# Global scores moved behind the local scores, on eight 64x32 parts, in the steady part of an attention and feed-forward kernel

## The chip, the cores and the metric

The kernel runs on one core of one Trainium2 chip (trn2). The metric is the device time of one execution in microseconds, lower is better. A core has TensorE (PE) for matmuls, with the loading of weights shown as an engine of its own (PEld), VectorE (DVE), ScalarE (ACT), GpSimd (POOL), and SyncE (SP), which issues the transfers.

## The reference

Attention over 8 batches and 8 heads with head size 64: 512 local tokens, which see the local keys within a window of 32 on either side and the 32 global keys, and 32 global tokens, which see all 544 keys. Its output is the input of a feed-forward stage with token shift (an RWKV channel mix), in float32.

```python
k_all = np.concatenate([k_g, k_l], axis=2)
v_all = np.concatenate([v_g, v_l], axis=2)
s_g = scale * np.matmul(q_g, k_all.transpose(0, 1, 3, 2))
out_g = np.matmul(sm(s_g), v_all)
...
s_l = np.concatenate([s_lg, s_ll], axis=-1)      # s_ll masked to the window
out_l = np.matmul(sm(s_l), np.concatenate([v_g, v_l], axis=2))
...
xk = mu_k * x + (1.0 - mu_k) * x_prev
xr = mu_r * x + (1.0 - mu_r) * x_prev
k = np.maximum(xk @ w_k, 0.0)
v = k * k @ w_v
r = 1.0 / (1.0 + np.exp(-(xr @ w_r)))
return r * v
```

## The kernel before

A unit is a batch and two neighbouring heads on 128 partitions (64 per head); two units make a pair, and a batch of eight heads is two pairs. The keys stand in 22 blocks of 32 (`ORDER`): after every three local blocks comes a copy of the global keys, so that a window of 128 columns holds three local blocks and the global one. The feed-forward stage multiplies float32 operands as two parts, high and low, in three products (`products`, L615). A feed-forward step is 24 matmuls of 256 columns into one PSUM bank (2 halves, 4 blocks, 3 products), or as many with the values' weights.

PSUM has eight banks. In the middle of the kernel (`MIDDLE_USE`, L132) three are used in turn under the name "m", four under "s" and one under "t". The feed-forward stage uses "m"; the local scores, weighted sums and part of the transposes use "s"; transposes and the smaller part of the global scores use "t".

The opening (`FIRST`, L66) is a list of steps by hand for batches 0 and 1 and the softmax of the first pair of batch 2; the pairs in it are called a to e. From batch 1 on `in_turn` (L970) takes turns, by a string of letters (`BATCH`, L1365), between attention steps ("A", for the pairs of the next batch) and feed-forward steps ("F"). The order of TensorE's instructions is that of the program (`in_line`), and so are those of VectorE, ScalarE and GpSimd (`manual_schedule`, L1209). Waits for tiles and banks are put in by the framework.

The attention steps of a pair are in `attention` (L925): transposes of the local probabilities of this pair, transposes of its global probabilities in two groups (`transposes_global`, L530), and behind the second group, in the same step, the local scores of the next pair (`scores`, L434, per unit: `make` L383 with 64 matmuls in all per pair on parts of 64 rows and 32 columns, then `read` L404 on VectorE). One or more feed-forward steps follow. The next attention step begins with the next pair's global scores (`Global.make`, L479): queries of both heads in a block-diagonal 128x64 operand, one matmul of 480 columns and one of 64 per unit, so that the two units stand on partitions 0 to 63 and 64 to 127. `Global.read` (L495) has VectorE take the smallest of the negated scores per row and copy. Behind that stand the weighted sums of this pair (`weighted`, L549; 56 matmuls of two passes). `exps`, `norm` and `soften` (L965) spread the exponentials and normalizations of the softmax over the feed-forward steps that follow.

A matmul of float32 operands appears in the trace as two instructions; the feed-forward parts are of type fp32r, and appear as one.

## Time and profile before

| | before |
|---|---|
| median of 3 runs | 630.09 us (629.71 to 630.24) |
| profiled execution, first to last instruction | 628.5 us |
| busy: TensorE | 620.1 us (99%) |
| busy: VectorE | 440.0 us (70%) |
| busy: ScalarE | 379.7 us (60%) |
| busy: GpSimd | 340.1 us (54%) |

The profiled execution is known by its span; what the runs' times hold beyond it (1.6 us of the median) lies before the first and behind the last instruction. Names in the rows are those of the program: `ps_s`, `ps_t` and `ps_m` are the banks, `raw_qk` holds a unit's queries and keys, `Pt` and `Pg` the local and global probabilities, `PT` their transposes, and `raw_v` the values. A matmul's line is that of a helper (L160 for matmuls, L163 for transposes), so blocks are told apart by tiles and shapes: 64*32 is a matmul on 64 rows and 32 columns of the array, and 128x480 moves 480 columns.

### The profile page before, as it was taken

The numbers are of one execution on the slowest core, as the hardware profiler recorded it, in microseconds if no ns is written. First come the engines' busy times: TensorE is split into PE (matmuls) and PEld (weight loads), VectorE is DVE, ScalarE is ACT, GpSimd is POOL, SyncE is SP. The second block draws the span as 40 slices with busy tenths as digits, with TensorE's granted clock in tenths as the row PEclk, the third lists the DMA queues.
The fourth block names the chain that finished last, engine by engine and source line by source line (L and its number), as shares of the span: only waits on it lengthen the run. The fifth ranks groups of instructions, "written<-read, shape, count | busy, mean of one in ns | idle before, by whom it ended". The sixth has DMA issues, their size and how long they took to land.

```text
span 628.5 us, 20469 instructions
## 1 busy us (share of the span) xinstructions
PE 620.1 (99%) x8356; PEld 590.7 (94%) x8356; DVE 440.0 (70%) x1227; ACT 379.7 (60%) x1147; POOL 340.1 (54%) x310
## 2 busy tenths in 40 slices
PE   8999999999999999999999999999999999999997
PEld 4689999999999999999999999999999999999997
DVE  7999983758888487676695677676696657345960
ACT  6899967164383768565857657665847744433531
POOL 8786455536846245846276535846275534543660
PEclk9999999999999999999999999999999999999999
DMA  8955562457383546276463928276463834377684
GB/s 337 408 197 217 193 224 82 169 183 273 118 305 131 201 139 236 60 269 235 158 248 108 378 75 335 88 267 228 162 243 104 299 117 137 105 222 246 200 261 142
DMA packets 43278, 127.29 MB, mean 203 GB/s; under 512 B 3760, under 2 KB 20656, under 8 KB 43184
## 3 DMA queue, kind: packets, MB, share of 16 engines
q1 hardware_dynamic: 43184, 125.98, 56.1%
q8 instruction: 66, 1.08, 0.7%
q14 instruction: 28, 0.23, 0.1%
HBM read 108.66 MB, written 17.30 MB: 200 GB/s over the span
## 4 chain that ended last, share of the span: by engine, by line
PE 85%; DVE 5%; DMA 3%; POOL 3%; ACT 2%; issue 1%; DVEq 0%; POOLq 0%; ACTq 0%
PE ps_m L160 65%; PE ps_s L160 13%; PE ps_t L163 4%; PE ps_t L160 2%; DMA w<-w_v 2%; ACT Pt L417 1%; PE ps_s L163 1%; DMA raw_qk<-qk 1%; POOL wv_l L271 1%; DVE a L299 1%; DVE diff L664 1%; POOL w L252 1%; POOL Pt L428 0%; DVE diff L659 0%; DVE xfull L664 0%
## 5 line engine op out<-in xcount | busy, mean ns | idle before, releaser
L160 PE MATMUL ps_m<-xkh,wk_h 128*128 128x256 f32 x544 | 154.1, 283 | 0.0
L160 PE MATMUL ps_m<-xkl,wk_h 128*128 128x256 f32 x544 | 150.5, 277 | 0.0
L160 PE MATMUL ps_m<-xkh,wk_l 128*128 128x256 f32 x544 | 150.5, 277 | 0.0
L160 PE MATMUL ps_m<-bh,a 128*128 128x256 f32 x736 | 131.7, 278 | 0.0
L428 POOL TENSOR_TENSOR Pt<-Pt,ssum 128x512 f32<-128x512 f32 x64 | 69.4, 1088 | 81.0 <-ACT Pt L417 38.9
L160 PEld LDWEIGHTS ps_m<-bh,a 128*128 128x128 f32 x736 | 113.1, 188 | 0.0
L417 ACT ACTIVATE Pt<-Pt,m 128x128 f32<-128x128 f32 x256 | 99.5, 395 | 14.4 <-DVE m L410 14.4
L160 PEld LDWEIGHTS ps_m<-xkh,wk_h 128*128 128x128 f32 x544 | 102.2, 188 | 3.7 <-issue 1.2
L160 PEld LDWEIGHTS ps_m<-xkh,wk_l 128*128 128x128 f32 x544 | 102.3, 188 | 0.0
L160 PEld LDWEIGHTS ps_m<-xkl,wk_h 128*128 128x128 f32 x544 | 102.2, 188 | 0.0
L160 PE MATMUL ps_m<-bl,a 128*128 128x256 f32 x368 | 101.7, 276 | 0.0
L160 PE MATMUL ps_m<-xrh,wr_h 128*128 128x256 f32 x272 | 76.7, 282 | 0.0
L702 ACT ACTIVATE relu<-ps_m 128x512 f32<-128x512 f32 x52 | 30.9, 595 | 74.3 <-PE ps_m L160 69.0
L669 POOL TENSOR_TENSOR xkl<-xfull,xkh 128x512 fp32r<-128x512 f32 x30 | 40.2, 1339 | 65.8 <-DVE ssum L361 33.6
L160 PE MATMUL ps_m<-xrl,wr_h 128*128 128x256 f32 x272 | 75.2, 277 | 0.0
L160 PE MATMUL ps_m<-xrh,wr_l 128*128 128x256 f32 x272 | 75.2, 276 | 0.0
L410 DVE CUSTOM_DVE_ANT_0 Pt<-ps_s,masks 128x128 f32<-128x128 f32 x256 | 55.9, 285 | 24.2 <-PE ps_s L160 24.2
L160 PEld LDWEIGHTS ps_m<-bl,a 128*128 128x128 f32 x368 | 69.2, 188 | 0.0
L669 POOL TENSOR_TENSOR xrl<-diff,xrh 128x512 fp32r<-128x512 f32 x30 | 41.5, 1383 | 41.8 <-DVE xrh L668 26.7
L788 DVE TENSOR_TENSOR bl<-B,bh 128x512 fp32r<-128x512 f32 x41 | 40.1, 992 | 27.6 <-ACT bh L787 27.4
L788 POOL TENSOR_TENSOR bl<-B,bh 128x512 fp32r<-128x512 f32 x35 | 47.8, 1387 | 19.1 <-ACT bh L787 11.4
L664 DVE SCALAR_TENSOR_TENSOR diff<-diff,mu_r_sb,xT 128x256 f32<-128x256 f32 x56 | 57.2, 1061 | 0.0
(154 smaller groups left out, 1477.3 us busy)
## 6 DMA issues: line engine op xcount, KB each, us to landing
a<-scratch SPq DMA_DIRECT2D x92, 512.0 KB, 4.8
raw_v<-v SPq DMA_DIRECT2D x32, 896.0 KB, 8.6
raw_qk<-qk SPq DMA_DIRECT2D x32, 628.0 KB, 5.0
out_l<-gate SPq DMA_DIRECT2D x32, 256.0 KB, 2.2
w<-w_k SPq DMA_DIRECT2D x8, 512.0 KB, 12.9
w<-w_v SPq DMA_DIRECT2D x8, 512.0 KB, 4.0
w<-w_r SPq DMA_DIRECT2D x4, 512.0 KB, 3.6
scratch<-wv_h SPq DMA_DIRECT2D x8, 256.0 KB, 2.7
```

What stands on the lines that cost most here:

```text
L160: return in_line(nc.tensor.matmul(*a, **kw))
L163: return in_line(nc.tensor.transpose(*a, **kw))
L252: nc.gpsimd.tensor_scalar(word(n, F32, 1), word(n, F32, 1), REBIAS, 1.0, op0=ALU.mult, op1=ALU.mult)
L271: nc.gpsimd.tensor_sub(part_of_weights(n, "l"), word(n, F32, 0), part_of_weights(n, "h").bitcast(F32))
L299: nc.vector.tensor_sub(s.bitcast(F32R), s, hs.bitcast(F32))
L410: nc.vector.tensor_tensor_reduce(out=self.Pt[:, i], in0=self.place(t, n, h), in1=masks[:, 2 * self.slots[t][1] + n], op0=ALU.add, op1=ALU. ...
L417: nc.scalar.activation(self.Pt[:, i], self.Pt[:, i], AF.Exp, bias=self.low_x[:, i:i + 1], scale=-1.0, accum_out=self.ssum[:, i:i + 1],)
L428: nc.gpsimd.tensor_mul(self.Pt[:, some], self.Pt[:, some], inv.unsqueeze(2).to_broadcast([P, 4, W]))
L664: nc.vector.scalar_tensor_tensor(self.shape(xf[:, j]), self.shape(d[:, j]), mu[:, c0 + j:c0 + j + 1], self.prev(c0 + j), op0=ALU.mult, op1 ...
L669: nc.gpsimd.tensor_sub(lo[:, both], xf, hi[:, both].bitcast(F32))
L702: nc.scalar.activation(rk, kp, AF.Relu)
L788: (by or (nc.vector if b[0] == "B" else nc.gpsimd)).tensor_sub(l, val, h.bitcast(F32))
```

## The change

From the second pair of batch 2 on (eleven pairs), the global scores are made by a new class, `GlobalByHalves`, directly behind the local scores of both units, in the same attention step; the feed-forward steps that stood between them now stand between the scores and the weighted sums alone. The keys are taken in two halves, and heads apart: a matmul has the 64 rows of one head, the 32 queries of one unit, and first 192, then 128 columns of keys, so eight matmuls of a round stand on eight different parts. The rows of a head's bank are then half, unit and query; the heads are in two banks, one under "t" and one under "m". The 128-column round overlaps between the halves and is masked with a constant (`twice`). Since a row's keys are in two partitions' rows, `both` combines the smallest values and the sums of the halves. The exponentials, normalizations and copies of the transposes are done per head; the transposes of the second group go to an "m" bank. VectorE's reads stand in the order: first unit's first bank, its second bank, the global scores, the second unit's two banks. The first pair keeps the old code. A few tiles get padding: `Pg` by 512 bytes, `twice` 1024 bytes, `other` 128 bytes in each of four buffers.

```diff
--- before.py
+++ after.py
@@ -52,6 +52,7 @@
 )
 QG = 2 * SG
+GK = 2 * (W - CK) + W
 K0 = QG + SL
 NV = 2 * NW * D
 TOK = 256
@@ -197,6 +198,7 @@
     nothing = const.tile([P, SL - CK], BF16, name="nothing")
     nc.gpsimd.memset(nothing, 0.0)
+    twice = const.tile([P, 512], BF16, name="twice")[:, :GK]
     PT = const.tile([P, 2, 2, PART], F32, name="PT")
@@ -493,9 +495,9 @@
                 matmul(out[j * QG:(j + 1) * QG], s.qk[:, 0:QG], keys, start=True, stop=True)
         def read(self):
-            self.Pg = att2.tile([P, NGK], F32, tag="Pg", name="Pg")
+            self.Pg = att2.tile([P, NGK + P], F32, tag="Pg", name="Pg")[:, :NGK]
             self.m = small.tile([P, 2], F32, tag="mg", name="mg")
-            self.ssum = small.tile([P, 1], F32, tag="ssumg", name="ssumg")
+            self.ssum = small.tile([P, 2], F32, tag="ssumg", name="ssumg")[:, 0:1]
             nc.vector.tensor_tensor_reduce(
                 out=self.Pg[:, FIRST_K:], in0=self.sp[1], in1=nothing[:, :NGK - FIRST_K], op0=ALU.add, op1=ALU.min,
                 scale=-scale, scalar=HUGE, accum_out=self.m[:, 0:1],
@@ -517,6 +519,87 @@
         def norm(self):
             self.inverse()
             self.normalize()
+    class GlobalByHalves:
+        def __init__(self, units):
+            self.units = units
+        def make(self):
+            self.sp = [psum("t"), psum("m")]
+            for at, n in ((0, 2), (2 * (W - CK), 1)):
+                for u, s in enumerate(self.units):
+                    for half in range(2):
+                        first = s.k[:, 2 * W * half:2 * W * half + W - CK] if n == 2 else (
+                            s.k[:, SK - W:] if half == 0 else s.k[:, SK - CK - W:SK - CK]
+                        )
+                        out = slice((2 * half + u) * SG, (2 * half + u + 1) * SG)
+                        for h in range(2):
+                            rows = slice(h * D, (h + 1) * D)
+                            keys, to = first[rows], self.sp[h][out, at:at + n * first.shape[1]]
+                            if n == 2:
+                                keys = bass.AP(keys.tensor, keys.offset, (keys.ap[0], (W, 2), (1, W - CK)))
+                                to = to.rearrange("p (t n) -> p t n", t=2)
+                            matmul(to, s.qk[rows, h * SG:(h + 1) * SG], keys, start=True, stop=True)
+        def both(self, x, op, tiny):
+            other = small.tile([P, 32], F32, tag="other", name="other")[:, :2]
+            for half in range(2):
+                there = x[(1 - half) * D:(2 - half) * D]
+                nc.vector.tensor_tensor(other[half * D:(half + 1) * D], there, there, op=ALU.max)
+            if tiny is None:
+                nc.vector.tensor_tensor(x, x, other, op=op)
+            else:
+                nc.vector.scalar_tensor_tensor(x, x, tiny, other, op0=ALU.add, op1=op)
+        def read(self):
+            self.Pg = att2.tile([P, NGK + P], F32, tag="Pg", name="Pg")[:, :2 * GK].rearrange("p (h n) -> p h n", h=2)
+            self.m = small.tile([P, 2], F32, tag="mg", name="mg")
+            self.ssum = small.tile([P, 2], F32, tag="ssumg", name="ssumg")
+            for h in range(2):
+                nc.vector.tensor_tensor_reduce(
+                    out=self.Pg[:, h], in0=self.sp[h][:, :GK], in1=twice, op0=ALU.add, op1=ALU.min,
+                    scale=-scale, scalar=HUGE, accum_out=self.m[:, h:h + 1],
+                )
+            self.both(self.m, ALU.min, None)
+        def exps(self):
+            for h in range(2):
+                nc.scalar.activation(
+                    self.Pg[:, h], self.Pg[:, h], AF.Exp, bias=self.m[:, h:h + 1], scale=-1.0,
+                    accum_out=self.ssum[:, h:h + 1],
+                )
+        def norm(self):
+            self.both(self.ssum, ALU.add, 1e-9)
+            nc.vector.reciprocal(self.ssum, self.ssum)
+            for h in range(2):
+                nc.gpsimd.tensor_scalar(
+                    self.Pg[:, h], self.Pg[:, h], self.ssum[:, h:h + 1], 1.0, op0=ALU.mult, op1=ALU.mult
+                )
+    def transposes_by_halves(Pg, h):
+        tp = psum("tm"[h])[:, :3 * P].rearrange("p (t n) -> p t n", n=P)
+        for n, at in enumerate((0, W - CK, 2 * (W - CK))):
+            size = W if n == 2 else W - CK
+            transpose(tp[:size, n], Pg[:, h, at:at + size], ident)
+        def place(rows, at, step, n):
+            first = PT[rows, 0, h, at:at + CK]
+            return bass.AP(first.tensor, first.offset, (first.ap[0], (step, n), (2 * PART, 2), (1, CK)))
+        for rows, half, ns, at, step in (
+            (slice(0, W - CK), 0, slice(0, 2), TAIL[0], TAIL[1] - TAIL[0]),
+            (slice(0, W - CK), 1, slice(0, 3), TAIL[2], CK),
+            (slice(D, P), 0, slice(2, 3), TAIL[5], CK),
+        ):
+            n = ns.stop - ns.start
+            nc.scalar.copy(
+                place(rows, at, step, n),
+                tp[rows, ns, half * D:(half + 1) * D].rearrange("p t (u q) -> p t u q", u=2),
+            )
     def cells(x, at, step, n, size=CK):
@@ -935,25 +1018,34 @@
                     for copy in done:
                         copy()
                     yield
-            transposes_global(Pg, 0)()
-            yield
-            transposes_global(Pg, 1)()
+            for part in range(2):
+                if pair is pairs[0]:
+                    transposes_global(Pg, part)()
+                else:
+                    transposes_by_halves(Pg, part)
+                if part == 0:
+                    yield
             if nxt:
-                R = [scores(whole(s)) for s in nxt]
+                R = [Scores(whole(s)) for s in nxt]
+                G = GlobalByHalves(nxt)
+                R[0].make()
+                R[0].read(0)
+                R[1].make()
+                G.make()
+                R[0].read(1)
+                G.read()
+                R[1].read(0)
+                R[1].read(1)
                 halves = list(product(R, range(2)))
                 halves[0][0].exps(0)
                 for (r, h), (r_next, h_next) in zip(halves, halves[1:]):
                     softmaxes.append((lambda r=r, h=h: r.norm(h), lambda r=r_next, h=h_next: r.exps(h)))
             yield
-            if nxt:
-                G = Global(nxt)
-                G.make("s", "t")
-                G.read()
-                Pg = G.Pg
             weighted(pair, True)()
             if nxt:
                 softmaxes.append((lambda: R[1].norm(1), G.exps))
                 softmaxes.append((G.norm,))
+                Pg = G.Pg
             for s in nxt or ():
                 load_v(s)
             yield pair[1].c + 1 == NC
@@ -1220,6 +1312,9 @@
         for s in pair_of["e"]:
             if not hasattr(s, "v"):
                 load_v(s)
+    nc.gpsimd.memset(twice, 0.0)
+    nc.gpsimd.memset(twice[:D, GK - W:GK - D], NEG)
+    nc.gpsimd.memset(twice[D:, GK - CK:], NEG)
     heads = attention(later_pairs, [group["e0"], group["e1"]], group_g["e"].Pg)
     leftp = sump = gate3 = None
     SUMS_AT = range(4, 20)
```

## Rows read from the trace of the kernel before

**Rows 1.** The page: span; TensorE busy time, share, instructions.
```profile
span 628.5 us, 20469 instructions
...
PE 620.1 (99%) x8356; PEld 590.7 (94%) x8356; DVE 440.0 (70%) x1227; ACT 379.7 (60%) x1147; POOL 340.1 (54%) x310
```

**Rows 2.** TensorE's waits, 126 to 500 us: total, times, longest.
```profile
PE ps_s L160 <- DVE m L410: 0.3, 1, 0.3
```

**Rows 3.** TensorE timeline, 474.7 to 478: start, length, line, operation, instructions.
```profile
475.42 2.06 PE L160 MATMUL ps_s<-raw_qk 64*32 64x128 f32 x128
477.40 0.38 PE L160 MATMUL ps_m<-xkh,wk_h 128*128 128x256 f32 x1
```

**Rows 4.** The same view, 482.6 to 488 us.
```profile
482.86 0.28 PE L160 MATMUL ps_m<-xkh,wk_l 128*128 128x256 f32 x1
483.06 0.34 PE L160 MATMUL ps_t<-raw_qk 128*64 128x64 f32 x4
483.23 0.98 PE L160 MATMUL ps_s<-raw_qk 128*64 128x480 f32 x4
484.03 3.63 PE L160 MATMUL ps_s<-PT,raw_v 128*64 128x96 f32 x112
487.59 0.39 PE L160 MATMUL ps_m<-xrh,wr_h 128*128 128x256 f32 x1
```

**Rows 5.** The same view, 516.9 to 521.5 us, the last pair.
```profile
517.28 0.28 PE L160 MATMUL ps_m<-xkh,wk_l 128*128 128x256 f32 x1
517.48 3.68 PE L160 MATMUL ps_s<-PT,raw_v 128*64 128x96 f32 x112
521.09 0.39 PE L160 MATMUL ps_m<-xrh,wr_h 128*128 128x256 f32 x1
```

**Rows 6.** Groups by form, 126 to 500: count, busy us, mean ns, idle.
```profile
L160 PE MATMUL ps_s<-raw_qk 128*64 128x480 f32 x44 | 10.8, 569 | 0.3 <-DVE m L410 0.3
```

**Rows 7.** TensorE timeline, 170.4 to 176.2 us, one pair.
```profile
171.00 0.34 PE L160 MATMUL ps_t<-raw_qk 128*64 128x64 f32 x4
171.60 1.03 PE L160 MATMUL ps_s<-raw_qk 128*64 128x480 f32 x4 [0.26 <-DVE m L410]
172.43 3.75 PE L160 MATMUL ps_s<-PT,raw_v 128*64 128x96 f32 x112
176.10 0.39 PE L160 MATMUL ps_m<-xkh,wk_h 128*128 128x256 f32 x1
```

**Rows 8.** Groups by form, 126 to 500 us, VectorE.
```profile
L410 DVE CUSTOM_DVE_ANT_0 Pt<-ps_s,masks 128x128 f32<-128x128 f32 x176 | 38.0, 285 | 21.9 <-PE ps_s L160 21.9
...
L503 DVE CUSTOM_DVE_ANT_0 Pg<-ps_s,nothing,mg 128x480 f32<-128x480 f32 x11 | 7.9, 718 | 2.7 <-PE ps_s L160 1.7
...
L361 DVE TENSOR_SCALAR ssum<-ssum 128x4 f32<-128x4 f32 x44 | 7.6, 173 | 3.4 <-ACT Pt L417 3.3
```

**Rows 9.** Groups by form, 126 to 500 us, ScalarE.
```profile
L509 ACT ACTIVATE Pg<-Pg,mg 128x544 f32<-128x544 f32 x11 | 8.1, 736 | 0.0
...
L540 ACT COPY PT<-ps_t 96x384 f32<-96x384 f32 x11 | 5.1, 465 | 0.0
```

**Rows 10.** Timeline of all engines, 294.5 to 304.5 us, VectorE and ScalarE.
```profile
294.60 0.69 DVE L888 TENSOR_TENSOR sum<-ps_m,sum 128x512 f32<-128x512 f32 x1 [0.83 <-PE ps_m L160]
...
297.66 0.60 ACT L702 ACTIVATE relu<-ps_m 128x512 f32<-128x512 f32 x1 [2.10 <-PE ps_m L160]
...
299.34 0.47 ACT L540 COPY PT<-ps_t 96x384 f32<-96x384 f32 x1
...
300.68 0.28 DVE L410 CUSTOM_DVE_ANT_0 Pt<-ps_s,masks 128x128 f32<-128x128 f32 x1
...
304.19 0.69 DVE L780 TENSOR_TENSOR B<-B,B 128x512 f32<-128x512 f32 x1
```

**Rows 11.** Engines by stretch: busy us (instructions) per engine, clock, DMA.
```profile
110.51:113.43 2.92, 2.92 (x28) 2.92 (x27) 2.88 (x7) 0.59 (x1) 0.00 (x0) 1.00 0.34 102
113.78:116.61 2.83, 2.83 (x28) 2.83 (x27) 2.73 (x5) 0.59 (x1) 1.23 (x1) 1.00 0.95 368
```

## The prediction

> **What bounds the kernel now.** I read the page first. Its first lines say that TensorE is busy for 620.1 of the 628.5 us of the span [rows 1]: this kernel ends when TensorE has got through its list, and the other engines count only where TensorE waits for them. So I looked at TensorE's waits next. In the stretch from 126 to 500 us, which holds all scores that the change touches, no wait on its list is longer than 0.3 us, and that one is for VectorE's reads of local scores [rows 2]. What is left to win is TensorE's own time. I therefore read its timeline block by block, always from the first start of one block to the first start of the next, because the modelled ends overlap.
>
> In a pair of units the local scores are 128 instructions (64 matmuls of two passes each) on eight 64x32 parts of the array, from 475.42 to 477.40 us [rows 3]. Two feed-forward steps later the global scores follow: 8 instructions on two 128x64 parts, from 483.06 to 484.03, and straight behind them the weighted sums, to 487.59 [rows 4]. The last pair has no global scores ahead of its weighted sums, so it shows what a feed-forward step followed directly by weighted sums costs: from 517.48 to 521.09 [rows 5]. The group of 480-column matmuls has 44 instructions in the stretch, four per block, so there are 11 such blocks [rows 6]. That is the number of pairs which the change touches; the earlier three pairs with this shape are in the hand-written opening and keep the old code.
>
> **Part by part: TensorE.** Removed, per pair: the block of global scores, 484.03 - 483.06 = 0.97 us [rows 4]. The 0.20 us between the last feed-forward matmul (482.86) and the block's first stays, for the weighted sums need the same change of parts: in the last pair it is 517.48 - 517.28 = 0.20 as well [rows 5]. What comes back is that the first weights of the sums are no longer loaded beside global scores: 3.61 us with no global block ahead [rows 5] against 3.56 with one [rows 4], so 0.05.
>
> Added, per pair: 16 matmuls of two passes, so 32 instructions, half of them on 192 columns and half on 128, behind the local scores and on the same eight parts. I take their pace from the local scores. Those take 1.98 us [rows 3], of which about 0.20 is the change back to the full array (as large as the 0.20 of [rows 4]), so 1.78 for 128 instructions: 13.9 ns for 128 columns on one of eight parts, or 0.87 ns for a column on one part (13.9 x 8 / 128). The old global block bears out that this is a rate of columns: two parts, each with 2 passes of 64 and 480 columns, 1088 columns in 0.97 us, or 0.89 ns each [rows 4]. The new block gives each part 2 x (192 + 128) = 640 columns: 640 x 0.88 = 0.56 us. Bounds: if the 13.9 ns were a rate of instructions, 32 x 13.9 = 0.45; if small matmuls cost what those of the weighted sums do, 3.36 us (3.56 less the change of parts) / 112 = 30 ns [rows 4], 32 x 30 = 0.96. I take 0.56, because these are the same kind of instruction on the same parts as in [rows 3], plus 0.02 once a pair, since the new code visits the four column parts in the order 0, 2, 1, 3 and the local scores in the order 0, 1, 2, 3. The change back to the full array is paid once, as now.
>
> The Trainium skill, page "TensorE: Matmul & The Clock Gate", section "Wait — 56ns, not 53.3ns?", has a rule against this change: start to start of matmuls is said never to fall under about 25 ns, however few columns they have. By it the new block would cost an estimated 32 x 25 = 0.8 us, and the gain would shrink to 0.12 us a pair, some 628.5 us in all. The trace does not agree for matmuls on separate parts: those of [rows 3] follow each other at 13.9 ns.
>
> The transposes of the global probabilities stay six per pair, with the same column sizes (two of 96 and one of 128 per group where they were 96, 96, 128 and 96, 96, 96); I cost this at nothing on TensorE.
>
> Net per pair: 0.97 - 0.05 - 0.56 - 0.02 = 0.34 us; for 11 pairs 3.7 us.
>
> **One pair is different.** At 171.00 the old global block takes 1.43 us (to 172.43) and its weighted sums 3.67 (to 176.10), because it needs a score bank that VectorE has not read yet: 0.46 and 0.11 us more than in a usual pair [rows 7]. VectorE reaches those reads late there, whatever TensorE does. In the new order no global matmul stands there, and the weighted sums come 0.6 us later to the same banks. They use three of the four banks of the local scores, in the order in which VectorE reads them; the third is read behind the new global reads (about 1.5 us, below), and may bring back up to 0.4 us. Of the 0.57 I count 0.3.
>
> **The other engines.** VectorE reads two banks of 320 columns instead of 64 and 480, and has three small operations more in the read and two more in the normalization. From 285 ns for 128 columns and 718 for 480 [rows 8], 320 columns take about 520 ns, some 0.45 from start to start; a small operation like the sum's takes 0.17 to 0.2. The new read is 2 x 0.45 + 3 x 0.2 = 1.5 us where the old was about 0.8, and with two more small operations VectorE gets about 1.1 us a pair. ScalarE gets six copies for three and two exponentials for one: with 465 ns for a copy of 384 columns and 736 for the exponential of 544 [rows 9], so some 0.3 for each smaller copy and 0.55 for each exponential of 320, about 1.0 us more. GpSimd normalizes two pieces for one and fills one small mask before the first of these pairs. None of this is on TensorE's path, if the following covers hold.
>
> What waits behind the moved reads: VectorE's queue is in order, so the second unit's reads, the next sums and the mixing come up to 1.5 us later, and are repaid by as much as the old read took when its place comes two steps on. The tightest case is a pair with three feed-forward steps before the weighted sums, such as that at 297 us [rows 10]. VectorE ends its sixteen reads at 304.2. The weighted sums come at about 309; 304.2 + 1.5 is well before that.
>
> What waits for banks: the new code takes two turns of the three "m" banks between two feed-forward steps. The transposes take one that VectorE emptied at 295.3, two microseconds before; the scores take the next. The feed-forward step behind them gets the bank that ScalarE's relu at 297.66 empties by 298.3; it starts at about 300.5 (297.5 + 0.4 + 2.0 + 0.6). The step after that needs the transposes' copies (299.34 and three in a row, by 300.2; needed at 303.3). The third needs the global read: VectorE starts at 300.68, has the first unit's eight reads done at 302.4 and the global ones at 303.9; needed at 306.1 [rows 10]. The smallest cover is 2.2 us. If it were gone, each lost microsecond would be a microsecond of the end, per pair.
>
> **The sum.** 3.7 + 0.3 = 4.0 us off the profiled span of 628.5 us. The runs have a median of 630.09; the 1.6 us between lie outside the span and stay. So 630.1 - 4.0 = 626.1 us.
>
> **Rivals.**
> (a) The columns aren't the limit of the new block. At 13.9 ns per instruction the pair gains 0.45 us: 11 x 0.45 + 0.3 = 5.2, so 624.9. For it: nothing in the trace tells a rate of columns from a rate of instructions in [rows 3] alone; against it: the agreement with the 480-column block.
> (b) Small matmuls cost 25 to 30 ns each: 0.80 to 0.96 us for the block, gain 0.12 down to nothing, 628.5 to 630.1. For it: the weighted sums; against it: the local scores.
> (c) A wait takes the place of the gain: the feed-forward step waits for an "m" bank behind VectorE's or ScalarE's longer queue. The pair of [rows 7] shows that VectorE can be late by several microseconds in the opening batches; three pairs that lose 0.7 us each give 628.2.
> (d) Slower: the pace of the feed-forward matmuls. Two steps of 24 matmuls that are alike take 2.92 and 2.83 us at the same granted clock of 1.00 [rows 11]: 0.09 us, or 4 ns of some 115 in each matmul, 3.2%. A step that starts at another moment, or a layout that isn't quite neutral, can move steps to the slower pace. Feed-forward is about 400 of the 502 us after 126 (the rest is twelve pairs of 8 to 9 us with their transposes); the gain is gone at 1.0% (4 us), and were all steps at the slow pace the time would be 639. A third of them gives 630.4. Against it: the change moves tiles by whole multiples of 512 bytes, and the pair of rows shows both paces in one kernel with one layout, so that the slow one is met already.
> (e) The change doesn't do what it says: TensorE empties the array between local and global scores for another 0.20 us a pair, so that they don't run as one block: 11 x 0.20 = 2.2, 628.3.
>
> **How the numbers follow.** Forecast 0.73; (a) 0.05; (b) 0.04; (c) 0.07; (d) 0.07; (e) 0.04. The forecast's own range is 625.2 to 627.2, from 0.02 to 0.06 us a pair of uncertainty and the late pair. To hold eight in ten it reaches to (c) and to (a): 624.9 to 628.3. A measurement of this kernel can tell about 0.2%, 1.3 us, so faster means under 628.8: the forecast, (a), (c) and (e), less some of (c), 0.87; within 0.2%: (b) and the mild part of (c) and (d), 0.07; slower 0.06.
>
> **What would show it.** Right: 160 instructions from the local scores' start to the feed-forward step, in about 2.55 us; feed-forward straight to weighted sums of 3.61; no new waits of TensorE. Wrong: more than 0.65 us between the end of the local scores and the end of the global ones; TensorE waiting for VectorE's global read or ScalarE's tail copies; a feed-forward step of 24 that takes 2.92 where it took 2.83.

## The result, and the profile after

The kernel got slower: 639.28 us (median; 637.27 to 640.23) against 630.16 us (629.71 to 631.26) for the kernel before on the same chip. The ratio is 1.0135, with a 95% interval of 1.0115 to 1.0155. Forecast were 626.1 us, in a range from 624.9 to 628.3. The profiled run of after took 640.23 us, with a span of 638.4.

First the page of after: its span, TensorE's busy time, and the queue that brings instructions. They answer to [rows 1].

```profile
span 638.4 us, 21079 instructions
...
PE 624.6 (98%) x8620; PEld 599.6 (94%) x8620; DVE 461.4 (72%) x1282; ACT 386.6 (61%) x1202; POOL 349.3 (55%) x324
...
q8 instruction: 68, 1.11, 0.7%
```

TensorE is still the bound, but there are now 13.8 us of the span in which it isn't busy; before there were 8.4.

The block that was moved does what was forecast. Below is TensorE's timeline of the pair that [rows 3] and [rows 4] show (start, length, line, operation, instructions).

```profile
485.06 2.01 PE L161 MATMUL ps_s<-raw_qk 64*32 64x128 f32 x127
486.83 0.32 PE L161 MATMUL ps_t<-raw_qk 64*32 64x192 f32 x1
486.84 0.32 PE L161 MATMUL ps_m<-raw_qk 64*32 64x192 f32 x1
...
487.39 0.27 PE L161 MATMUL ps_m<-raw_qk 64*32 64x128 f32 x1
487.59 0.38 PE L161 MATMUL ps_m<-xkh,wk_h 128*128 128x256 f32 x1
```

Local and global scores run as one block of 2.53 us, where the local scores alone took 1.98 [rows 3]: 2.529 less 1.986 to the nanosecond, so 0.54 for the 32 new instructions (forecast: 0.56). The weighted sums behind feed-forward last 3.61 us, as in [rows 5]. So the move itself gives 0.97 - 0.54 - 0.05 = 0.38 us a pair. The loss is elsewhere, in two places.

**First, feed-forward is slower behind the weighted sums.** Engines by stretch (length, busy time and instructions of each engine, granted clock, DMA share and rate), the three double steps of 48 matmuls behind the weighted sums of this pair. The kernel before:

```profile
487.59:493.16 5.57, 5.57 (x51) 5.57 (x50) 3.06 (x5) 3.82 (x17) 2.47 (x2) 1.00 1.01 397
493.95:499.49 5.54, 5.54 (x52) 5.54 (x50) 2.35 (x5) 4.41 (x9) 3.48 (x3) 1.00 0.62 206
500.28:505.82 5.54, 5.54 (x52) 5.54 (x51) 4.85 (x7) 2.68 (x5) 4.17 (x4) 1.00 0.41 146
```

and after:

```profile
496.86:502.62 5.76, 5.76 (x51) 5.76 (x50) 4.25 (x8) 3.81 (x17) 2.48 (x2) 1.00 1.01 396
503.41:509.16 5.75, 5.75 (x52) 5.75 (x51) 2.21 (x4) 4.76 (x11) 3.47 (x3) 1.00 0.70 217
509.95:515.69 5.74, 5.74 (x52) 5.74 (x50) 5.48 (x7) 2.67 (x5) 4.92 (x5) 1.00 0.45 163
```

The clock is 1.00 in all six (2.4 GHz of its levels of 1.2 and 2.4), and so is the work. Start to start, feed-forward matmuls follow each other at 113.3 ns before and at 117.7 ns after. It is the pair of paces of [rows 11]. A run of matmuls keeps one or the other.

**Second, TensorE stops inside some score blocks.** TensorE's three longest waits between 126 and 500 us (waited for, total, times, longest), where the kernel before has the one of [rows 2] and another of 0.3 us for ScalarE's copies:

```profile
PE ps_s L161 <- issue: 1.9, 1, 1.9
PE ps_t L161 <- issue: 1.6, 2, 0.9
PE ps_m L161 <- DVE m L412: 1.2, 1, 1.2
```

"Issue" means that nothing in the profile released the instruction. One of these stops on the timeline, in the fourth pair:

```profile
237.15 0.27 PE L161 MATMUL ps_m<-raw_qk 64*32 64x128 f32 x1
238.29 0.27 PE L161 MATMUL ps_t<-raw_qk 64*32 64x128 f32 x1 [0.87 <-issue]
```

Eight matmuls before the end of the block nothing starts for 1.14 us, though their operands and banks are those of the matmuls just before. Five of the eleven blocks take longer than 2.53 us: 3.77, 4.75, 3.77, 3.61 and 2.67 us, 5.9 us in all.

The stop in the third pair has a sequel in this run alone. Behind 2.15 us with hardly any matmul the granted clock falls to 0.51, the level of 1.2 GHz, for 3.4 us:

```profile
203.75:205.90 2.15, 0.27 (x20) 0.02 (x2) 2.15 (x17) 1.41 (x7) 1.24 (x1) 1.00 0.37 122
206.00:207.20 1.20, 1.20 (x54) 1.00 (x54) 0.09 (x1) 0.14 (x2) 0.00 (x0) 1.00 0.08 18
207.20:210.60 3.40, 3.40 (x17) 3.40 (x17) 3.24 (x25) 0.00 (x0) 0.00 (x0) 0.51 0.73 205
211.00:213.00 2.00, 2.00 (x53) 1.87 (x52) 0.00 (x0) 1.26 (x3) 0.76 (x1) 1.00 0.59 236
```

Sixteen matmuls take 213 ns each there, which costs 1.6 us. The three other runs of after have a mean clock of 1.000 and spans of 635.4 to 637.9 us.

The ledger, from the first local scores of the first pair to those of the eleventh (10 pairs; 348.9 us before, 358.6 after), worked out from the starts of TensorE's instructions:

```
the moved block, 10 x -0.38                                   -3.8
stops inside score blocks                                     +5.9
slow pace: 1268 starts at 117.7 ns where there were 248       +4.6
half clock behind the third stop                              +1.6
the pair at 172 us: its weighted sums still wait for a bank   +0.2
rest: TensorE waits of 0.1 to 0.35 us                         +1.2
sum                                                           +9.7
```

### The profile page after: what moved, and what is told of

The parts are those of the page before. It is cut to its first block, busy times and chain, and to the rows that moved or that the text cites. A ratio compares the mean times of both kernels' runs of the same rounds, so it can differ in the third digit from the quotient of the medians.

```text
span 638.4 us, 21079 instructions
## 1 busy us (share of the span) xinstructions
PE 624.6 (98%) x8620; PEld 599.6 (94%) x8620; DVE 461.4 (72%) x1282; ACT 386.6 (61%) x1202; POOL 349.3 (55%) x324
## 3 DMA queue, kind: packets, MB, share of 16 engines
q8 instruction: 68, 1.11, 0.7%
## 4 chain that ended last, share of the span: by engine, by line
PE 80%; DVE 6%; POOL 3%; DMA 2%; issue 2%; ACT 2%; SPq 0%; DVEq 0%; POOLq 0%; ACTq 0%
PE ps_m L161 65%; PE ps_s L161 10%; PE ps_t L164 3%; DMA w<-w_v 1%; PE ps_s L164 1%; DMA raw_qk<-qk 1%; PE ps_t L161 1%; DVE a L301 1%; POOL wk_l L273 1%; PE ps_m L164 1%; POOL Pt L430 1%; DVE Pt L412 1%; POOL w L254 1%; ACT Pt L419 0%; DVE diff L747 0%
## 5 line engine op out<-in xcount | busy, mean ns | idle before, releaser
L161 PE MATMUL ps_m<-bh,a 128*128 128x256 f32 x736 | 134.5, 281 | 0.0
L161 PEld LDWEIGHTS ps_m<-bh,a 128*128 128x128 f32 x736 | 114.5, 189 | 0.0
L161 PE MATMUL ps_m<-bl,a 128*128 128x256 f32 x368 | 103.1, 280 | 0.0
L747 DVE SCALAR_TENSOR_TENSOR diff<-diff,mu_r_sb,xT 128x256 f32<-128x256 f32 x56 | 53.4, 993 | 0.0
```

The source lines that it names most:

```text
L161: return in_line(nc.tensor.matmul(*a, **kw))
L747: nc.vector.scalar_tensor_tensor(self.shape(xf[:, j]), self.shape(d[:, j]), mu[:, c0 + j:c0 + j + 1], self.prev(c0 + j), op0=ALU.mult, op1 ...
```

## The experiments

The two theories to be told apart from chance and from each other:

- **Pace.** The pace of feed-forward is a state with two values. Weighted sums straight behind feed-forward turn it; with global scores in between it stays. The move took the global scores out of there.
- **Instruction supply.** TensorE's instructions come in packets of 16 KB: in the page's row above, 68 packets and 1.11 MB. The trace has 17,424 instructions of TensorE (17,240 matmuls and weight loads, and 184 that wait for semaphores or drain), so 256 for a packet. The block of after has 160 of each, 320 instructions at 7 ns, where the local scores alone had 256. It runs through more than a packet in one go, faster than the next one comes.

The rivals: the operands' addresses (the layout) set the pace; the stops are waits for what other engines do in those pairs.

The first six runs below (up to "How many instructions turn the pace") have one time each, beside a single 632.15 us of the kernel before on the same chip (span 630.4). The kernel before has taken 629.6 to 632.96 us beside one run or another, so a difference of a microsecond or two in these times shows little by itself; what such a run shows is read from its trace.

### Two small matmuls ahead of the weighted sums

```diff
+        if lead:
+            for h in range(2):
+                matmul(sums[0][h * D:(h + 1) * D, 0:CK], units[0].v[:, h, 0], ident[:, 0:CK], start=True, stop=True)
         groups(0, shared)
```

> The changed kernel with two small matmuls (128x64 weights, 32 columns, overwritten at once) ahead of the weighted sums of the eleven pairs, in the place where the old global scores stood. Theory P (the slower pace of the feed-forward steps comes from how TensorE enters the weighted sums: with another matmul on the same parts ahead of them the first feed-forward matmul comes out on the fast pace): the steps of 48 behind the weighted sums go from 5.76 to 5.56 us, those between the transposes from 5.74 to 5.54, some 0.6 us a pair in the eight later pairs, so about 5 us off the 638 us span: 633, plus or minus 1.5 for the stalls inside the score blocks. Rival A (the pace comes from the moved tiles' addresses): 5.76 and 5.74 stay, 638 to 640. Rival B (the pace comes from the transposes into an 'm' bank or the busier engines): stays, too.

Measured: 635.15 us, span 633.4. The number fits and the reason doesn't. The sums with the two matmuls ahead turned the pace like those without: behind them it changed in ten of eleven cases, three of them from slow to fast. The span is 5.0 us shorter than that of after because the stops took 3.4 us less (blocks of 3.72, 2.74, 3.24, 2.77 and 2.68 us), no half clock followed (1.6), and 1054 starts were slow where after has 1481 (1.9); against that, the two matmuls cost 0.12 us a pair, and the first block began 0.8 us later. Not any small matmul will do.

### The old global block, moved

```diff
-                G = GlobalByHalves(nxt)
+                G = Global(nxt)
...
-                G.make()
+                G.make("m", "t")
```

> Only the move: the old global scores, 8 instructions on two 128x64 parts, stand directly behind the local scores, with the old transposes, softmax and mask. Theory P: feed-forward then weighted sums, so the slow pace is there: 5.76 us for 48 behind the weighted sums, as in the changed kernel. Theory F (stalls come where more than 256 instructions of TensorE follow at full pace, because instructions arrive in pieces of 16 KB): the block is 272 instructions long, so at most two of the eleven blocks stall, at the sixth and seventh pair, by under 0.5 us. Sum: 630 + 5 (pace) + 11 x 0.25 (one more change of parts and the unhidden first weights) = 637 to 639. Rival (stalls come from the banks that the moved scores take, or from VectorE's reads): the four stalls of over 1 us in the first five pairs stay.

Measured: 636.13 us, span 634.3. This block has 272 instructions, 3.06 us in each of the eleven pairs: none stopped. The pace was slow nearly as often as in after (1208 of 3503 starts at 116 ns or more, 5.5 us over 113.3 ns a start; after has 1481 of 3482). So the two losses are separate, and the slow pace needs no eight parts, only the move. The span is under the 637 to 639 us expected, and no stop was in that sum: it took 630 as its base where the span of before is 628.5, 5 us for the pace where the slow starts beyond those of before make 4.0, and 0.25 us a pair for the move where 3.06 - 1.99 - 0.97 + 0.05 = 0.15 were needed. With these, 628.5 + 4.0 + 11 x 0.15 = 634.2.

### The same program, its instructions moved by 136

```diff
+            if True:
+                for half in range(2 * n):
+                    matmul(bank[:, half % 8 * D:(half % 8 + 1) * D], ident, ident[:, 0:D], start=True, stop=True)
+                return
             k = min(n, 4)
```

The fillers of the opening are cut in halves, which makes 136 TensorE instructions more; the rest of the program is that of after.

> The changed kernel with 34 small filling matmuls more in the hand-written opening (136 instructions of TensorE), made by splitting the fillers that are there; nothing else is touched. Theory F: the borders of the 256-instruction pieces move by 136 towards the start in every score block; the stalls of the first, third, fourth and fifth pair (1.2, 2.2, 1.2, 1.1 us) go, and new ones of up to 1.3 us come in the ninth and tenth pair, where the border then falls some 25 to 30 instructions into the block. Span about 4 us shorter, 634 plus or minus 1.5. Rival (banks, VectorE's late reads or the loads of the next pair): the same four pairs stall as before, span 638 plus up to 1.

Measured: 638.29 us, span 636.5. The opening became 4.1 us longer (the first block starts at 130.6 where it was 126.5), which was not counted; without it the span is 632.4. The stops in the blocks moved to where they were expected, out of pairs 1, 3, 4 and 5 and into pairs 9 and 10. The third pair was not free of them: its block took 2.74 us, and its weighted sums stood still for 1.34 us at 215.84 us, three matmuls before their end, where TensorE waited for "issue" as well. Engines by stretch, five of the blocks (pairs 1, 4, 5, 9 and 10):

```profile
130.59:133.12 2.53, 2.53 (x162) 2.33 (x160) 1.26 (x5) 1.47 (x3) 0.00 (x0) 1.00 0.19 61
235.78:238.31 2.53, 2.53 (x162) 2.33 (x160) 0.86 (x3) 2.21 (x6) 1.16 (x1) 1.00 0.24 31
270.18:272.71 2.53, 2.53 (x162) 2.33 (x161) 1.34 (x13) 2.46 (x9) 2.53 (x3) 1.00 0.03 6
411.37:414.67 3.30, 2.85 (x162) 2.35 (x161) 1.78 (x16) 3.23 (x12) 2.44 (x2) 1.00 0.36 76
446.24:449.03 2.79, 2.79 (x162) 2.28 (x161) 1.21 (x2) 2.11 (x6) 0.00 (x0) 1.00 0.28 94
```

Nothing about the work of pairs 9 and 10 had changed, only their instructions' numbers.

### The kernel before, with a block of 320

```diff
-                R = [scores(whole(s)) for s in nxt]
+                R = [scores(whole(s), s is nxt[1]) for s in nxt]
...
+        if again:
+            r.make(only=0)
```

Half of the second unit's local scores are computed twice, so that the block has 320 instructions without any of the change.

> The kernel before with 16 of the second unit's 64 local score matmuls made twice in each of the eleven pairs, so that the block has 320 instructions, as long as the changed kernel's; global scores, banks and everything else stay as before. By itself 16 matmuls cost 0.22 us a pair, 2.5 us. Theory F: stalls of about 1 us inside some of these blocks, at the first and, by the count of instructions, at the ninth and tenth pair; span 628.5 + 2.5 + 2 to 4 = 633 to 635, and the feed-forward pace stays the fast one. Rival (the moved scores' banks or reads cause the stalls): none, 631.

Measured: 636.42 us, span 634.6. The blocks take 2.42 us, but 3.40 in the first pair and 3.09 in the ninth; the tenth, which was expected to stop too, did not. The pace stayed that of before: fast behind the weighted sums in ten of the eleven pairs. That the span lies in the expected 633 to 635 is in part luck: a block became 0.44 us longer and not 0.22, and one stop fewer made up for some of it. But stops came where none of the change was there.

### The eight parts alone, at the old place

```diff
-                G.make()
                 R[0].read(1)
-                G.read()
...
+            if nxt:
+                G.make()
+                G.read()
             weighted(pair, True)()
```

> The eight-part global scores at the old place, between the feed-forward steps and the weighted sums; nothing is moved. Instruction supply: the score block has 256 TensorE instructions again and the global part has 64, so no score block should take over 2.0 us and the first block stays at 1.99 us. The global block should take 0.56 us in place of 0.97 us. Pace: the weighted sums have small matmuls ahead of them again, as in the kernel before. If it is their presence ahead of the sums that lets the feed-forward behind them run at 113.3 ns, the span is 628.5 - 11 x 0.41 = 624.0 us (623 to 626). If the new form turns the pace as the sums alone do, the 48 feed-forward matmuls behind the sums take 5.76 us and the span is 628.5 - 4.5 + 5 = 629 us (628 to 631).

Measured: 631.35 us, span 629.6. No block stopped, and the pace behind the sums was fast in all pairs. The global block took 0.70 us, because a change of parts of 0.2 us lies between it and the sums. Beside the sums' 0.05 that leaves 0.22 us a pair, 2.4 us in all. Against the kernel before on the same chip the span fell by 0.8 us, against the 628.5 us of the trace of before it rose by 1.1, so the time doesn't tell whether the 2.4 arrived. The trace shows where some of it went: the first block begins 0.5 us later than in the trace of before, in four batches TensorE waits 0.34 to 0.6 us more for GpSimd's low parts, 1.6 us in all, and in the third pair it waits 0.7 us more than before. The suspect for the low parts is the second normalization on GpSimd, which had been costed at nothing.

### How many instructions turn the pace

```diff
             weighted(pair, True)()
+            if nxt:
+                fill_narrow(psum("t"), (4, 1, 2, 3)[at % 4])
```

One to four transposes of the identity, behind the weighted sums.

> The kernel after with one, two, three or four 128x128 transposes of the identity behind the weighted sums, by pair (4, 1, 2, 3, 4, 1, ...). If the pace is a state of two values that the weighted sums turn, and that four transposes turn again (the trace of before has 16 such turns at four transposes and none at eight), the 48 feed-forward matmuls behind sums and four transposes take 5.56 us in pairs 1, 5 and 9, where the kernel after has 5.76; one, two and three transposes tell what the turn depends on. If the pace has to do with where the operands lie or with the moved scores, all pairs keep 5.76 us. The cost is 0.1 us a transpose, so 0.1 to 0.4 us a pair; the span 636 to 640 us, by where the score blocks come to stall.

Measured: 638.86 us, span 637.1. Engines by stretch, the two double steps of feed-forward (48 matmuls, with 8 transposes between them) that follow the sums, for one, two, three and four transposes in turn:

```profile
316.70:322.24 5.54, 5.54 (x49) 5.54 (x50) 5.35 (x12) 4.01 (x19) 2.76 (x2) 1.00 0.97 363
323.04:328.57 5.53, 5.53 (x51) 5.53 (x50) 5.31 (x9) 3.65 (x6) 3.79 (x4) 1.00 0.77 283
351.39:356.94 5.55, 5.55 (x51) 5.55 (x51) 3.86 (x7) 3.75 (x17) 2.48 (x2) 1.00 1.02 414
357.73:363.47 5.74, 5.74 (x52) 5.74 (x51) 2.19 (x4) 4.77 (x11) 3.48 (x3) 1.00 0.70 217
388.30:393.84 5.54, 5.54 (x52) 5.54 (x50) 5.36 (x11) 3.80 (x18) 2.77 (x2) 1.00 0.99 373
394.63:400.38 5.75, 5.75 (x52) 5.75 (x51) 5.53 (x10) 3.65 (x7) 4.02 (x4) 1.00 0.65 238
423.01:428.75 5.74, 5.74 (x52) 5.74 (x51) 3.63 (x7) 3.52 (x15) 2.47 (x2) 1.00 1.02 412
429.54:435.28 5.74, 5.74 (x51) 5.74 (x50) 2.19 (x4) 4.77 (x11) 3.48 (x3) 1.00 0.60 191
```

One transpose makes both steps fast; it costs 0.085 us. Two and three help only up to the next eight transposes, and four do not help at all, against what was expected of them. The layout is the same in all these rows, and so are the steps: the rival that blames addresses alone is out.

### One transpose behind the sums

```diff
+            if nxt and at >= 3:
+                fill_narrow(psum("t"), 1)
```

> The kernel after with one 128x128 transpose of the identity behind the weighted sums of the eight later pairs, and nothing else. If the slow pace is a state that the weighted sums turn and one transpose turns back (pairs 2, 6 and 10 of the run with one to four transposes showed it, behind other counts in the pairs before), all eight pairs should run 5.54, 5.54 and 5.54 us of feed-forward in place of 5.76, 5.74 and 5.74, for 0.085 us of the transpose: 8 x (0.62 - 0.085) = 4.3 us off. The stalls in the score blocks stay (1.0 to 1.3 us in the first and fourth pair, 2.2 us about the third). Span 631 to 634 us where the kernel after has 635.4 to 638.4. If the three pairs owed it to the counts around them, the span stays above 635 us.

Measured: 635.05 us in one run, beside 630.55 for the kernel before on the same chip (median of seven), span 633.3. Feed-forward behind the sums takes 5.54 us in all eight later pairs, and all their double steps are fast: 491 slow starts are left, where after has 1481. The stops stayed, 4.06, 4.28, 3.10 and 2.88 us in pairs 1 and 4 to 6. The pace theory stands.

### The same, moved

```diff
+            if n == 5:
+                for i in range(38):
+                    h, u = 0, i % 4
+                    matmul(bank[u * SG:(u + 1) * SG, 256 * h:256 * h + CK], ident[h * D:(h + 1) * D, 0:SG],
+                           ident[h * D:(h + 1) * D, 0:CK], start=True, stop=True)
             k = min(n, 4)
```

> The run before with 38 small matmuls (76 TensorE instructions) in the opening, where TensorE waits for the first inputs. If the stalls in the score blocks are TensorE out of instructions at a border of 256 of them, at the places counted in the trace of after less 76 and less 2 a pair from the fifth, no block has a border at its instructions 20 to 64 or 276 to 320, and all eleven blocks take 2.53 us (the last perhaps 0.2 more, the third 2.75 as in three runs so far). That is 5 us less than the run before, less 0 to 0.6 us for the matmuls: span 626 to 629 us. If the stalls are due to what the other engines do at that time, they stay, and the span is 630 to 634 us.

Measured: 636.31 us, ratio 1.0093 (1.0077 to 1.0110), span 634.1. Nine blocks run through in 2.53 us, but the third takes 4.03 and the eighth 4.18, and just behind the seventh there is a stop of 0.73. The mistake was in the count: each of these matmuls has two passes and two weight loads, so the program moved by 152 and not by 76. To see what the count says, all of TensorE's instructions in the trace (matmuls, weight loads, and those that wait for semaphores or drain) are numbered here by their start, from 0; "place" is how many of the block stand ahead. For some of the stops, the instruction that comes late:

```
kernel                 pair  place in block  number  remainder  late by  packet's end to the start
after                   1        321          4033      193      1.25 us    1.38 us
after                   3        215          6081      193      2.15       1.41
after                   4        306          7105      193      1.14       1.21
after                   5        297          8129      193      1.03       1.32
two small matmuls       4        282          7105      193      0.58       1.54
moved by 136            9        297         12481      193      0.71       1.28
moved by 136           10        288         13505      193      0.30       1.40
block of 320            9        296         12481      193      0.61       1.54
moved by 152            3        319          6337      193      1.27       1.23
moved by 152            8        320         11457      193      1.70       1.52
```

The remainder is that of the number divided by 256. In all runs together 25 starts of this kind in or just behind a score block of 320 instructions are late by over 0.26 us. Each has the remainder 193, and each comes 1.2 to 1.55 us after a packet of the instruction queue has landed. Blocks of 256 or 272 instructions have such numbers at the same distance from their start, but behind their end, and are never late there. From the previous instruction with that remainder to the late one it is 2.2 to 3.6 us in these rows (6.4 in the second), while 256 instructions of such a block take 1.9. Nowhere in the fifteen traces does an instruction with this remainder, late or not, start less than 1.2 us after its own packet has landed. That is the cause of the stops: the next 256 instructions are not there yet. It is not bound to score blocks: the 1.34 us in the weighted sums of the run moved by 136 came at number 6593, remainder 193, 1.5 us after its packet. The table's first row is one that the list of waits puts down to VectorE's read.

The Trainium skill, page "Runtime: NRT & Kernel Launch", section "Instruction fetch mechanics", says that each engine's instructions are refilled in blocks of 16 KiB or 256 instructions, while the previous block runs, and that this stays hidden because engines issue more slowly than the blocks are filled. The trace agrees with the size. It does not agree that the refill is hidden where an engine takes an instruction every 7 ns for longer than a block.

### One normalization on VectorE

```diff
-                nc.gpsimd.tensor_scalar(
+                (nc.vector, nc.gpsimd)[h].tensor_scalar(
```

On top of the run before.

> The run before with one of the two normalisations of the global softmax on VectorE in place of GpSimd, which has 2 x 755 ns of it a pair where the kernel before has 937 ns. If TensorE's waits of 0.2 to 0.7 us in each batch for GpSimd's low parts come of that longer queue, they go, and the span is 1 to 2.5 us under the run before, 625 to 627 us. If GpSimd isn't the reason, or VectorE becomes late in its place, the span is the same within 0.5 us or longer by up to 2 us.

Measured: 634.76 us, ratio 1.0069 (1.0052 to 1.0085), span 632.7, 1.4 us less. The waits for GpSimd became shorter but did not go, and the third and the eighth block stopped again, at the same numbers.

### The count mended

```diff
-                for i in range(38):
+                for i in range(20):
```

The run before with 20 matmuls, 80 instructions.

> The run with three changes, with 20 small matmuls in place of 38. Each of them turned out as four TensorE instructions, so 38 moved the borders by 152 and not by 76. In all runs so far every stall in a score block lies at a TensorE instruction whose number, counted from the start of the program, leaves 193 when divided by 256; with 20 matmuls (80 instructions) such an instruction stands at places 16 to 241 of the eleven blocks and none at 276 to 321. Instruction supply: all eleven blocks 2.53 us, span 632.7 - 3.2 - 0.3 = 629.2 us (628.5 to 630.5), level with the kernel before. If the stalls belong to the third and eighth pair for another reason, they stay, and the span is 632 to 633 us.

Measured: 633.72 us, ratio 1.0032 (1.0020 to 1.0044), span 630.1. All blocks take 2.53 us, but the third 2.74. One stop is left, just behind the tenth block, at its place 327 (number 13505, remainder 193), 1.17 us. Supply stands; the idea that pairs 3 and 8 are special falls. The profiled execution is the fastest of seven, at 631.95 us; the six others took 633.3 to 634.1, and what they lost isn't known.

### The eight parts at the old place, one normalization on VectorE

```diff
-                nc.gpsimd.tensor_scalar(
+                (nc.vector, nc.gpsimd)[h].tensor_scalar(
```

On top of the run with the eight parts at the old place.

> The eight-part scores at the old place, with one of the two normalisations of the global softmax on VectorE in place of GpSimd. In the run without that, TensorE waited 0.72, 0.46, 0.45 and 0.46 us for GpSimd's low parts, where a gap is else 0.115 us. If the second 755 ns on GpSimd is the reason, these 1.6 us go, and the span is 629.6 - 1.6 = 628 us (627.3 to 628.7), 0 to 0.2% under the kernel before. If not, it stays at 629.6 us or more.

Measured: 634.46 us, ratio 1.0049 (1.0032 to 1.0066), span 633.2. Three of the four waits for the low parts went, as expected, and yet the time rose. The score block now left the pace slow in five of the eleven pairs, where without this edit it did in none, and the sums behind global scores kept it: 1269 slow starts where there had been 357, 4.0 us. What turns the pace at the end of a score block I don't know.

### The change from the fourth pair on only

```diff
-            if nxt:
+            if nxt and at < 3:
+                R = [scores(whole(s)) for s in nxt]
+            elif nxt:
                 R = [Scores(whole(s)) for s in nxt]
                 G = GlobalByHalves(nxt)
...
+            if nxt and at < 3:
+                G = Global(nxt)
+                G.make("s", "t")
+                G.read()
             weighted(pair, True)()
```

The first three pairs keep the old code; the others have the transpose and the normalization on VectorE, and 9 small matmuls stand in the opening.

> The global scores in the old two-part form at the old place for the first three pairs, and behind the local scores in eight parts from the fourth on, with the transpose behind the weighted sums, one normalisation on VectorE, and 9 small matmuls in the opening, so that no block from the fourth on has an instruction with remainder 193 at its places 24 to 64 or 276 to 321. If what was found so far is all there is, the eight later pairs take 0.378 us less each for the move and pay 0.085 us for the transpose, and the waits at 172 and 201 us are those of the kernel before: 628.5 - 8 x 0.29 + 0.3 for the opening = 626.5 us (625.5 to 628), 0.2 to 0.4% under the kernel before. If waits for GpSimd's low parts of up to 1 us a batch stay, 628 to 630 us.

Measured: 632.95 us, ratio 1.0024 (1.0011 to 1.0037), span 631.3. One stop of 1.58 us came at place 324, just behind a block, and one of 0.32 at 335; that the danger reaches some 25 instructions past the block had been overlooked. Of the 4.8 us above the 626.5 expected these are 1.7; slow starts beyond those of the kernel before are 1.2 (excess 2.7 for 1.5 us), a wait for the low parts 0.5. A first block that begins at 127.1 for 126.5 is another 0.3, for 0.3 had been counted, and the fourth pair's block of 2.74 us another 0.2. The other 0.9 I couldn't place.

### No normalization on GpSimd

```diff
-                nc.gpsimd.tensor_scalar(
+                nc.vector.tensor_scalar(
```

On the run with 20 small matmuls, with 17 in their place.

> As the aligned run, with both normalisations of the global softmax on VectorE (387 ns each there) and none on GpSimd, which loses 937 ns a pair against the kernel before, and with 17 small matmuls in place of 20: the aligned run still had one stall of 1.17 us at an instruction with remainder 193, at place 327 of the tenth block's count, just behind its 320; with 17 such instructions stand at 79 or more, or at 28 or less. If GpSimd's queue is what the waits for the low parts (1.0, 0.15, 0.42 and 0.17 us) come from, they go: span 630.1 - 1.7 - 0.8 = 627.6 us (626.8 to 628.8), 0 to 0.3% under the kernel before. If VectorE, at three quarters busy, is late by the added 0.77 us a pair, waits for its reads and sums take their place: 629 to 632 us.

Measured: 630.31 us against 630.98, ratio 0.999 (0.9979 to 1.0001), span 628.4. All of the loss of after is gone; a gain is not shown, since the interval holds 1. Two things changed against the run before it, the normalization and the number at which instructions run out. In the two profiles the waits for the low parts went from 1.1 to 0.5 us and the one late instruction from 1.17 to 0.58; the time alone doesn't tell them apart. TensorE's longest waits in this run, 126 to 500 us:

```profile
PE ps_s L161 <- PE ps_m L161: 0.6, 1, 0.6
PE ps_m L161 <- POOL bl L871: 0.5, 1, 0.5
PE ps_m L161 <- issue: 0.3, 1, 0.3
```

The first is the pair at 172 us, which still waits for a bank, the third one more late instruction (13505 again, now at place 345). Of the 3.8 us which the moved block gives, these waits (1.4), the eight transposes (0.7), slow starts beyond those of before (0.5) and a first block that begins 0.5 us later use up most.

## Why the prediction was wrong

**The costs of the moved block were right.** Block 0.54 us (0.56 forecast), sums 0.05 more, no second change of parts between local and global scores. That decides three rivals: (e) fell, since the block has no break; (b) fell, 0.54 and not 0.80 to 0.96; and (a) fell the other way, 0.54 and not 0.45. It is a rate of columns: 640 on a part in 0.54 us are 0.85 ns each. The sentence on the Trainium skill's 25 ns and its 628.5 us falls with (b).

**The step that failed first is "3.61 with no global block ahead, so 0.05".** It priced the weighted sums by their own length [rows 5] and didn't ask what the next feed-forward step looks like. The answer stood right behind that row, in the same pair of the kernel before. TensorE's timeline there:

```profile
521.90 0.28 PE L160 MATMUL ps_m<-xrh,wr_h 128*128 128x256 f32 x1
522.02 0.28 PE L160 MATMUL ps_m<-xrl,wr_h 128*128 128x256 f32 x1
522.14 0.28 PE L160 MATMUL ps_m<-xrh,wr_l 128*128 128x256 f32 x1
522.26 0.28 PE L160 MATMUL ps_m<-xrh,wr_h 128*128 128x256 f32 x1
```

These start every 0.12 us, while behind the global block of a usual pair they start every 0.113. The only sums without global scores ahead after the opening were followed by the slow pace. The right term was 0.05 + 0.60 us for a later pair (three times 0.20), more than the 0.34 that the move was to bring.

**Rival (d) named the pace and had it wrong in cause and chance.** It gave 630.4 for a third of the steps; in after 1481 of 3482 starts are slow, 43%, and the excess over 113.3 ns is 6.7 us where it was 1.5. The size was right. But I took [rows 11] as a sign that the pace is an accident of moment or layout, gave it 0.07, and never tabulated what stands ahead of fast and slow runs. (The prediction's last sign of being wrong, slow feed-forward steps where they had been fast, is what came.) Over all fifteen traces, from 98 us on, the table is plain (from one run of feed-forward matmuls to the next; undecided ones left out):

```
between two runs of feed-forward      pace turned   pace kept
8 transposes                                4          236
4 transposes                              232            7
weighted sums alone                        62           11
old global scores + weighted sums           2           22
weighted sums + 1 transpose          fast behind 51 of 51
```

For the kernel before alone it says: four transposes turn (16 of 16), eight keep (16 of 16), global scores and sums keep (10 of 10, one undecided), sums alone turn once and keep once. That could have been read before the prediction. Two things don't fit a state that is only turned or kept. The four exceptions among the eight transposes are all in the run with one to four transposes. And behind three transposes of global probabilities alone, which the table leaves out, the pace was fast in 179 of 192 cases: 43 came from the slow one, and a fast one was lost once.

**No step had the stops; that is the second failure.** The trace of before shows none, since its longest run at 7 ns an instruction is 256. The prediction counted columns and durations and never instructions. The one sign was the count itself: 32 matmuls and 32 weight loads more, in one go with 256. Their 5.9 us in the profiled run are the largest item of the loss.

**The pair at 172 us.** 0.3 us were to come back and 0.34 to be won. Measured: 0.30 of waiting, 4.06 for the sums and 0.54 for the block, 4.90 where [rows 7] has 5.10. So 0.20 came of 0.64; the bank that VectorE reads late is late for the sums as well, as the prediction had put it for "up to 0.4".

**GpSimd at nothing.** "None of this is on TensorE's path" was wrong where GpSimd also makes the low parts that TensorE takes next. Its groups of the normalization between 229 and 500 us, before and after:

```profile
L515 POOL TENSOR_SCALAR Pg<-Pg,ssumg 128x544 f32<-128x544 f32 x8 | 7.5, 936 | 3.6 <-DVE ssumg L362 3.6
L578 POOL TENSOR_SCALAR Pg<-Pg,ssumg 128x320 f32<-128x320 f32 x16 | 12.6, 797 | 7.7 <-DVE ssumg L576 7.7
```

Two of 797 ns are 0.66 us a pair more. In after that shows little; I take it that TensorE is late itself there, which is not shown. With the pace mended, TensorE waits 1.3 us in all for the low parts with both normalizations on GpSimd, 0.9 and 1.1 with one (the two runs with 38 and 20 small matmuls), 0.5 with none. With one, GpSimd has no more of it than in the kernel before, so the length of its queue is a part of the cause and not all. With none the row is

```profile
L578 DVE TENSOR_SCALAR Pg<-Pg,ssumg 128x320 f32<-128x320 f32 x14 | 4.8, 384 | 0.2
```

**Rival (c)**, a feed-forward step that waits for an "m" bank, did not show: the covers of [rows 10] held.

What stays open: why the pace has two values and what in the array they are; why two small matmuls, or four transposes, don't do what one transpose does; why the score block sometimes ends in the slow one; why TensorE still waits for GpSimd where that has less to do than before; and why a few packets start late (in the third pair of after 3.2 us behind the previous instruction with that remainder, where the three others took 0.3 to 0.7).

## What to carry to other kernels

Where one engine bounds a kernel, price a removed block by what its neighbours do without it: look up, in the same trace, every place where the two neighbours already meet, and read on past them. Count instructions as well as time; a stretch of tiny matmuls longer than one refill of 256 can run dry, and whether it does depends on the number at which it starts, so an unrelated edit far ahead moves it. And when a gain doesn't come, mend the suspected losses one by one: here the transpose for the pace took the ratio to the kernel before from 1.0135 to about 1.007 (one run), and moving the stops and relieving GpSimd took it on to 0.999.

## What the runs showed of the hardware

- Feed-forward matmuls of 256 columns with a weight load each run at 113.3 or at 117.7 ns start to start, at a granted clock of 1.00, and keep the one they have until other work turns it. One 128x128 transpose of 0.085 us behind the weighted sums sets the fast one in 51 of 51 cases.
- TensorE can wait for its own instructions: up to 2.15 us at numbers with one fixed remainder of 256. From 126 us on, 25 of 26 such stops were in or just behind blocks that take an instruction every 7 ns for more than 256 of them. The list of waits calls that "issue", or gives it to an engine that had long been done.
- 192-column and 128-column matmuls on eight 64x32 parts cost 0.85 ns for a column of one part, 17 ns from start to start.
- After 2.15 us with hardly any matmul the granted clock was 1.00 for another 1.2 us and then 0.51 for 3.4 us.
